# Six marks in a table of twenty for a half-array score product, with new planner numbers and reordered first and last transfers, in a fused attention and gated feed-forward kernel

## The chip, the cores and the metric

The kernel runs on one core of one Trainium2 chip. The metric is the device time of one execution in microseconds; for the kernel before it is the median of three timed runs. One further execution was recorded by the hardware profiler, and all rows below are from that one.

The engines: TensorE (PE; its weight loads are shown apart as PEld), VectorE (DVE), ScalarE (ACT), GpSimd (POOL) and SyncE (SP), which here only issues transfers. Each engine works through its own list of instructions in a fixed order.

## The reference

```python
scores = scale * np.matmul(q, k.transpose(0, 1, 3, 2))      # 8 batches, 8 heads, 576 x 64; scale = 1/8
thresh = np.max(scores, axis=-1, keepdims=True) - tau
scores = np.where(scores >= thresh, scores, -1000000000.0)
scores = scores - np.max(scores, axis=-1, keepdims=True)
attn = np.exp(scores)
attn = attn / (np.sum(attn, axis=-1, keepdims=True) + 1e-09)
attn_out = np.matmul(attn, v)
...
x = attn_out with the heads side by side                     # 8 x 576 x 512
h = np.maximum(x @ w_in, 0.0)                                # 1024 channels
conv_out = a depthwise convolution of h over 3 neighbouring tokens (conv_w)
gate = 1.0 / (1.0 + np.exp(-conv_out))
return h * gate @ w_out                                      # 8 x 576 x 512
```

All in float32.

## The kernel before, in words

**Tiling.** A batch has 576 query rows: four tiles of 128 and one of 64. They form two chunks, tiles 0 and 1, and tiles 2, 3 and 4. The eight heads are taken as four pairs. A *unit* is one tile of one pair; a batch has 20 units, 8 in its first chunk and 12 in its second, and in every odd pair the tiles of a chunk are walked backwards. `unit` makes the scores of both heads in PSUM (tiles `ps_s`, two buffers, one head each), then the largest score of a row (DVE, `top`), the exponential (ACT, `exp`), a limit (`limit`), the mask with the row's sum (DVE, `mask`), a few small steps on the sums, and the normalisation (`norm`, POOL). `transposes` turns the result on PE (tiles `ps_t`), ACT copies it out to `eT`, and `attend` multiplies by v: first a product on quarters of the array (`mixed`), then four on halves of its columns. From batch 1 on, `attend` does two pairs together.

**Precision.** Batch 0 computes its scores in plain float32, on halves of the array's rows (line 537). Later batches split q and k into upper and lower bits (`q1`, `q2`; k's upper bits of a head stand in 64 partitions of `ks` and its lower bits in the other 64) and multiply with 128 rows: `q1` and `q2` each meet the upper and the lower bits of k at once (line 544, four products of 288 columns per head). The 64-row tile stays in float32 (line 537) in every batch.

**Feed-forward.** `mm1` multiplies a chunk's 256 or 322 columns by w_in (line 713, three products per 128 rows), DVE, ACT and POOL make convolution and gate, and a lower-bit rest `gl` is written by `low`. `mm2` multiplies 128 tokens by w_out (line 786). The feed-forward of a chunk is spread over the units of the next chunk. The weights come in 16 pieces of 512 KB, and each is rounded by ACT, POOL and three DVE instructions (lines 372 to 378).

**What sets the order.** Every step is given to a planner (`Plan`) with an engine, an assumed duration, a rank less an `AHEAD` value, and a kind. The planner walks through time and writes, engine by engine, a fixed order. Some steps may go to another engine if the backlog of their own is above `BACKLOG`. For PE it prefers a step of the kind that ran last (`rows`: halves or quarters of the array's rows; `cols`: halves of its columns; `turn`: transposes; `full`), within the limits in `KEEP`. So a change of one number can move instructions everywhere.

**Start and end.** The first pair's k comes in two parts on ACT's queue, its q in two parts on SP's queue, and three weight pieces follow on ACT's queue. At the end `mm2` of the last 128 tokens is copied out by ACT in one piece, and SP stores it.

## Time and profile before

| what | value |
|---|---|
| timed runs | 1109.76, 928.27, 928.84 us; median 928.84 us |
| the profiled execution's own time | 925.54 us |
| its span | 923.8 us |
| PE, DVE, ACT, POOL busy | 97%, 80%, 76%, 63% of the span |
| instructions | 19667 |

The span is the time from the first to the last instruction in the trace; 1.7 us of the execution's own time lie outside it. Busy shares are averages over the whole span: they say which engine is worth a look, and not where it waits.

### The profile page before, as it was taken

To read this page: it belongs to the slowest core of one execution; us is meant where nothing else is said; L and a number is where in the kernel's file an instruction comes from. 1 tells how busy PE (TensorE), PEld (TensorE's weight loads), DVE (VectorE), ACT (ScalarE), POOL (GpSimd) and SP (SyncE) were. 2 spreads that over 40 slices of the span, in tenths; PEclk is the share of its full clock that TensorE was granted. 3 is DMA by queue.
4 is the path that set the end of the run, shared out by engine and by line. 5 is a ranking of instruction groups with operands and counts; after the bars stand their busy time and mean duration, and the time that the engine had idled before them with its cause. 6 is when DMAs were issued, how large, how long until landed. Compare 5 with 4: busy or idle time off the path is not lost.

```text
span 923.8 us, 19667 instructions
## 1 busy us (share of the span) xinstructions
PE 896.7 (97%) x6308; PEld 731.8 (79%) x6308; DVE 741.1 (80%) x1853; ACT 701.2 (76%) x1590; POOL 582.1 (63%) x1028
## 2 busy tenths in 40 slices
PE   5989899999999999999999999999999999999998
PEld 2446588878889788879888787887888888887897
DVE  5988999979868798878967789886977879896643
ACT  5888898878678787869768687786958788785653
POOL 3665887767747586666746677675865757664422
PEclk9999999999999999999999999999999999999999
DMA  6643363355341652345423453416523265221000
GB/s 211 200 151 128 97 166 101 111 146 167 87 122 40 176 150 83 84 115 140 122 91 81 133 148 103 120 59 166 161 85 95 55 175 140 83 79 60 13 24 34
DMA packets 77926, 104.02 MB, mean 113 GB/s; under 512 B 18560, under 2 KB 49536, under 8 KB 77824
## 3 DMA queue, kind: packets, MB, share of 16 engines
q1 hardware_dynamic: 76960, 100.86, 38.6%
q10 hardware_dynamic: 864, 1.90, 0.6%
q8 instruction: 51, 0.84, 0.4%
q14 instruction: 51, 0.42, 0.1%
HBM read 58.88 MB, written 9.44 MB: 74 GB/s over the span
## 4 chain that ended last, share of the span: by engine, by line
PE 79%; ACT 9%; DVE 6%; issue 2%; DMA 2%; POOL 1%; SPq 0%; ACTq 0%; POOLq 0%; DVEq 0%
PE po L786 21%; PE ph L713 16%; PE ps_t L626 13%; PE pa L685 12%; PE ps_s L544 11%; PE ps_s L537 4%; ACT eT L621 2%; PE pa L676 2%; DVE em L564 2%; ACT em L561 2%; DVE few L552 1%; DVE t L748 1%; PE pw_stage L394 1%; DMA q<-in_qd_dram 1%; ACT hp L728 1%
## 5 line engine op out<-in xcount | busy, mean ns | idle before, releaser
L597 POOL TENSOR_SCALAR em<-em,few 128x576 f32<-128x576 f32 x285 | 258.3, 914 | 36.9 <-DVE few L588 27.3
L564 DVE SCALAR_TENSOR_TENSOR em<-ps_s,few,em 128x576 f32<-128x576 f32 x288 | 228.1, 812 | 51.0 <-ACT em L561 44.9
L713 PE MATMUL ph<-x,w1h 128*128 128x322 f32 (+1 forms) x1024 | 243.2, 305 | 0.7 <-ACT hp L728 0.7
L552 DVE TENSOR_REDUCE few<-ps_s 128x1 f32<-128x576 f32 x288 | 210.8, 748 | 29.4 <-PE ps_s L537 15.2
L561 ACT ACTIVATE em<-ps_s,few 128x576 f32<-128x576 f32 x288 | 206.7, 743 | 30.9 <-DVE few L552 26.0
L621 ACT ACTIVATE eT<-ps_t 128x512 f32<-128x512 f32 (+2 forms) x416 | 203.3, 512 | 16.9 <-PE ps_t L626 15.2
L626 PE MATMUL ps_t<-ident,em 128*128 128x128 f32 x1312 | 187.7, 276 | 4.6 <-DVE x L695 1.7
L626 PEld LDWEIGHTS ps_t<-ident,em 128*128 128x128 f32 x1312 | 152.3, 141 | 34.2 <-POOL em L597 11.0
L713 PEld LDWEIGHTS ph<-x,w1h 128*128 128x128 f32 x1024 | 174.9, 189 | 3.7 <-issue 1.8
L748 DVE SCALAR_TENSOR_TENSOR t<-hp,cw,t 128x255 f32<-128x255 f32 (+1 forms) x256 | 151.9, 597 | 25.9 <-ACT t L732 18.8
L544 PE MATMUL ps_s<-ks,q 128*128 128x288 f32 x896 | 155.0, 304 | 2.6 <-DVE em L564 1.6
L713 PE MATMUL ph<-x,w1l 128*128 128x322 f32 (+1 forms) x512 | 151.1, 295 | 0.0
L544 PEld LDWEIGHTS ps_s<-ks,q 128*128 128x128 f32 x896 | 129.0, 188 | 13.8 <-issue 4.6
L324 POOL TENSOR_TENSOR gl<-t,gh 128x255 fp32r<-128x255 f32 (+9 forms) x192 | 121.4, 644 | 29.4 <-ACT gh L765 29.2
L685 PE MATMUL pa<-eT,v 128*64 128x320 f32 (+1 forms) x1024 | 133.3, 412 | 0.0
L685 PEld LDWEIGHTS pa<-eT,v 128*64 128x64 f32 x1024 | 70.9, 138 | 59.9 <-issue 16.7
L786 PE MATMUL po<-w2h,gh 128*128 128x512 f32 x288 | 118.1, 410 | 0.0
L786 PE MATMUL po<-w2h,gl 128*128 128x512 f32 x288 | 113.0, 392 | 0.5 <-POOL gl L324 0.5
L786 PE MATMUL po<-w2l,gh 128*128 128x512 f32 x288 | 113.1, 393 | 0.0
L713 PEld LDWEIGHTS ph<-x,w1l 128*128 128x128 f32 x512 | 96.6, 189 | 0.1
L755 DVE SCALAR_TENSOR_TENSOR t<-t,hp 128x321 f32<-128x321 f32 (+1 forms) x128 | 70.8, 554 | 14.3 <-ACT t L757 13.6
L757 ACT ACTIVATE t<-t 128x321 f32<-128x321 f32 (+1 forms) x128 | 56.9, 445 | 24.4 <-DVE t L748 24.1
(69 smaller groups left out, 1019.6 us busy)
## 6 DMA issues: line engine op xcount, KB each, us to landing
q<-q SPq DMA_DIRECT2D x336, 64.0 KB, 2.0
v<-in_vc_dram SPq DMA_DIRECT2D x64, 288.0 KB, 3.3
k<-in_kp_dram SPq DMA_DIRECT2D x35, 320.0 KB, 3.6
out_dram<-ot SPq DMA_DIRECT2D x36, 256.0 KB, 2.0
xk<-in_kt_dram SPq DMA_DIRECT2D x28, 288.0 KB, 3.3
ks<-xk SPq DMA_DIRECT2D x56, 144.0 KB, 2.4
xq<-in_qt_dram SPq DMA_DIRECT2D x56, 128.0 KB, 2.3
stage<-in_w_out_dram SPq DMA_DIRECT2D x8, 512.0 KB, 3.5
```

The costliest lines, as they stand in the source:

```text
L324: engines[e].tensor_tensor(dst, x, y, op=ALU.subtract)
L544: nc.tensor.matmul(ps[:, c, :CH], lhsT=q[:, h, o:o + n], rhs=k[:, h, c * CH:(c + 1) * CH], start=(i == 0), stop=(i == 1))
L552: nc.vector.tensor_reduce(few[:rows, nm], ps[:rows, :, :CH], op=ALU.max, axis=mybir.AxisListType.XY, negate=True)
L561: nc.scalar.activation(view(), ps[:rows, :, :CH], AF.Exp, bias=few[:rows, nm])
L564: nc.vector.scalar_tensor_tensor(view(), ps[:rows, :, :CH], few[:rows, th], view(), op0=ALU.is_ge, op1=ALU.mult, accum_out=few[:rows, total])
L597: engines[e].tensor_scalar(sl, sl, by, to, op0=ALU.mult, op1=ALU.add)
L621: "act", act(w, True), lambda dst=dst, src=src: nc.scalar.activation(dst(), src(pt), AF.Copy),
L626: nc.tensor.transpose(out=pt[:, at:at + P], in_=em[:, int(b * P):int(b * P) + P], identity=ident[:])
L685: nc.tensor.matmul(pa[j * D:(j + 1) * D, :w], lhsT=vt[:, blk, :], rhs=eT[:, blk, :w], start=False, stop=(r == 3))
L713: nc.tensor.matmul(ph[:, :an], lhsT=w1[w][:, cb, fs], rhs=xs[cb][:, h, :an], start=(cb == 0 and i == 0), stop=(cb == NCB - 1 and i == 2))
L748: nc.vector.scalar_tensor_tensor(t[:, :kn], hp[:, k:kn + k], cw[:, 3 * f + k:3 * f + k + 1], t[:, :kn], op0=ALU.mult, op1=ALU.add)
L786: nc.tensor.matmul(po[:], lhsT=x[:, f, at:at + P], rhs=w[:, f, :], start=(f == 0 and i == 0), stop=(f == NFB - 1 and i == 2))
```

## The change

It has four parts.

**The half-array product.** A table `ROWS` of 20 marks, one for each unit of a batch, has six ones. Where a mark is set and the unit has split q and k, `q1` meets k as before (`mm_high`, two products per head), and `q2` meets only the upper bits of k (`mm_low`): four products on 64 of the array's rows, the two heads on different halves. The product of the two lower parts is left out there. Both `ps_s` buffers are begun before `mm_low` closes them. The ones stand at places 1, 4, 9, 11, 15 and 16. At places 10, 11, 16 and 17 of a batch the unit is the 64-row tile, which has no split q, so the marks at 11 and 16 do nothing: the built program has 112 instructions of `mm_low` (line 553), which is 28 units, four in each of seven batches.

**First transfers.** The second part of the first pair's k goes to SP's queue, between the two parts of q; all weight pieces go to SP's queue.

**Last output.** The last 512 columns are copied out in two halves, by ACT and DVE, and stored by ACT's and SP's queues.

**Planner numbers.** `AHEAD`, `BACKLOG`, `ALT`, `KEEP`, `MOE`, `TAP` and `LOW` have new values, with separate ones (`AHEAD0`, `BACKLOG0`) for the first 24 ranks. `NORM` names DVE in its first entry, which `NEAR = 0` never reads. In the built program this moves 25 of the `gl` subtractions (`low`) and 38 of the small steps on the sums from POOL to DVE; 32 first convolution taps (`tap0`) from POOL to ACT; 18 limits from DVE, and 19 from ACT, to POOL; and 3 normalisations from ACT to POOL.

```diff
-AHEAD = {'s': 6.25, 's4': 7.75, 't': 3.5, 'a': 3.5, 'prep': 4.25, 'w': 2.5, 'load': 7.75}
+
+AHEAD = {'s': 6.25, 's4': 7.25, 't': 4.25, 'a': 4.0, 'prep': 5.0, 'w': 2.0, 'load': 8.0}
+AHEAD0 = {'s': 6.25, 's4': 7.75, 't': 3.5, 'a': 3.5, 'prep': 3.0, 'w': 2.5, 'load': 8.75}
+HEAD = 24
...
-TAP = ('act', 'pool', 'act', 'act')
-LOW = ('pool', 'pool')
+TAP = ('act', 'act', 'act', 'act')
+LOW = ('pool', 'pool', 'pool', 'dve')
...
-MOE = (2, 2)
-BACKLOG = {'pool': 6860.0, 'dve': 120.0, 'act': 9000000000.0}
+MOE = (2, 1)
+BACKLOG = {'pool': 19208.0, 'dve': 60.0, 'act': 9000000000.0}
+BACKLOG0 = {'pool': 13720.0, 'dve': 120.0, 'act': 9000000000.0}
...
-ALT = 11.76
+ALT = 5.88
...
+ROWS = (0, 1, 0, 0, 1, 0, 0, 0, 0, 1, 0, 1, 0, 0, 0, 1, 1, 0, 0, 0)
...
-KEEP = {'rows': 2.304, 'cols': 1.613, 'turn': 3.226, 'full': 2.304}
+KEEP = {'rows': 2.304, 'cols': 1.613, 'turn': 4.516, 'full': 2.304}
...
-            for j, on in enumerate((slice(0, CH), slice(CH, S + D))):
-                op(
-                    "act", 450, lambda on=on: nc.scalar.dma_start(k[:, on], kp[b, p, :, on]), w=[(k, j)], ahead=210 - 10 * j,
...
+            op("act", 450, lambda: load_k(nc.scalar, first), w=[(k, 0)], ahead=210, late=LATENCY["sp"] + 700)
+            op("sp", 700, lambda: load_q(0), w=[(q, 0)], ahead=210, late=700)
+            op("sp", 800, lambda: load_k(nc.sync, second), w=[(k, 1)], ahead=209, late=500)
+            op("sp", 600, lambda: load_q(1), w=[(q, 1)], ahead=208, late=500)
...
+        pss = [plan.buf(ps_s, "ps_s", 2, [P, 2, 512], F32, f"ps_s_{u}_{h}") for h in range(m)]
+
+        side = q2 is not None and ROWS[u % len(ROWS)]
+        if side:
+
+            def mm_high(h):
+                for c in range(2):
+                    nc.tensor.matmul(
+                        pss[h][:, c, :CH], lhsT=q1[:, h, o:o + n], rhs=k[:, h, c * CH:(c + 1) * CH], start=True, stop=False
+                    )
+
+            def mm_low():
+                for c in range(2):
+                    for h in range(2):
+                        on = slice(h * D, (h + 1) * D)
+                        nc.tensor.matmul(
+                            pss[h][:, c, :CH], lhsT=q2[on, h, o:o + n], rhs=k[on, h, c * CH:(c + 1) * CH], start=False, stop=True
+                        )
+
+            for h in range(2):
+                op(
+                    "pe", 267, lambda h=h: mm_high(h), w=[(pss[h], 0)], r=[(x, (h, i)) for x in (k, q1) for i in range(2)], ahead=a,
+                    kind="full"
+                )
+            op("pe", 267, mm_low, w=[(ps, 0) for ps in pss], r=[(x, (h, h)) for x in (k, q2) for h in range(2)], ahead=a, kind="rows")
...
+        x, y = slice(0, DO // 2), slice(DO // 2, DO)
+        op("act", act(DO // 2, True), lambda: nc.scalar.activation(ot[:, x], po[:, x], AF.Copy), w=[(ot, 0)], r=[(po, 0)])
+        op("dve", dve(DO // 2), lambda: nc.vector.tensor_copy(ot[:, y], po[:, y]), w=[(ot, 1)], r=[(po, 0)])
+        op("act", 450, lambda: nc.scalar.dma_start(rows[:, x], ot[:, x]), r=[(ot, 0)], late=LATENCY["sp"])
+        op("sp", sp(DO // 2), lambda: nc.sync.dma_start(rows[:, y], ot[:, y]), r=[(ot, 1)])
```

**How the order moves, first place.** SP's queue at the very start of the program, before (`k_1`, `q1_1`, `v_1` are of the second pair; `stage` is a weight piece):

```order
L460 DMA q1_0_79<-in_qd_dram 128x256 x2
L451 DMA k_1_96<-in_kp_dram 128x640
L363 DMA stage_3_107<-in_w_in_dram 128x512
L452 DMA q1_1_124<-in_qd_dram 128x2x256
L513 DMA v_0_130<-in_vc_dram 128x576
```

and now:

```order
L466 DMA q1_0_79<-in_qd_dram 128x256
L463 DMA k_0_77<-in_kp_dram 128x352
L466 DMA q1_0_79<-in_qd_dram 128x256
L373 DMA stage_0_97<-in_w_in_dram 128x512
L373 DMA stage_1_107<-in_w_in_dram 128x512
L373 DMA stage_2_119<-in_w_in_dram 128x512
L373 DMA stage_3_131<-in_w_in_dram 128x512
L458 DMA k_1_150<-in_kp_dram 128x640
L459 DMA q1_1_160<-in_qd_dram 128x2x256
```

The first pair's second part of k stands second, and four weight pieces now stand ahead of the second pair's k.

**Second place.** PE in batch 0, where the fourth pair's product with v begins, before (`ps_t` are transposes, `pa` the product with v, `k_381` the next pair's k):

```order
L626 MATMUL ps_t_4_480<-ident,em_375 128x128 x4
L626 MATMUL ps_t_8_491<-ident,em_292 128x128
L626 MATMUL ps_t_8_491<-ident,em_375 128x128
L676 MATMUL pa_510<-eT_435,v_298 64x256 x2
L537 MATMUL ps_s_0_516<-k_381,q_4_400 128x288 x2
L537 MATMUL ps_s_1_523<-k_381,q_4_400 128x288 x2
L685 MATMUL pa_510<-eT_435,v_298 64x256 x8
```

and now:

```order
L664 MATMUL ps_t_4_479<-ident,em_384 128x128 x4
L573 MATMUL ps_s_1_486<-k_268,q_3_283 128x288 x2
L664 MATMUL ps_t_8_495<-ident,em_334 128x128
L664 MATMUL ps_t_8_495<-ident,em_384 128x128
L573 MATMUL ps_s_0_505<-k_413,q_4_460 128x288 x2
L714 MATMUL pa_514<-eT_447,v_321 64x256 x2
L723 MATMUL pa_514<-eT_447,v_321 64x256 x8
```

One score product now stands between the last transposes and the product with v that reads them.

**Third place.** PE in batch 4, around a joint product with v of two pairs, before (line 544 is the score product, line 713 `mm1`):

```order
L544 MATMUL ps_s_1_5971<-ks_1_5650,q_33_5709 128x288
L544 MATMUL ps_s_1_5971<-ks_1_5650,q_33_5729 128x288
L676 MATMUL pa_5976<-eT_5611,v_5601 64x320 x2
L676 MATMUL pa_5979<-eT_5744,v_5627 64x320 x2
L685 MATMUL pa_5976<-eT_5611,v_5601 64x320 x8
L685 MATMUL pa_5979<-eT_5744,v_5627 64x320 x8
L626 MATMUL ps_t_0_6042<-ident,em_5770 128x128 x4
L713 MATMUL ph_5_6052<-x_4800,w1h 128x256
```

and now, at a marked unit (lines 545 and 553 are `mm_high` and `mm_low`):

```order
L545 MATMUL ps_s_1_5856<-ks_0_5679,q_32_5489 128x288 x2
L553 MATMUL ps_s_0_5845<-ks_0_5679,q_32_5514 128x288
L553 MATMUL ps_s_1_5856<-ks_0_5679,q_32_5514 128x288
L553 MATMUL ps_s_0_5845<-ks_0_5679,q_32_5514 128x288
L553 MATMUL ps_s_1_5856<-ks_0_5679,q_32_5514 128x288
L714 MATMUL pa_5870<-eT_5595,v_5562 64x320 x2
L714 MATMUL pa_5873<-eT_5687,v_5577 64x320 x2
L723 MATMUL pa_5870<-eT_5595,v_5562 64x320 x8
L723 MATMUL pa_5873<-eT_5687,v_5577 64x320 x8
L664 MATMUL ps_t_0_5931<-ident,em_5814 128x128 x4
L580 MATMUL ps_s_0_5940<-ks_1_5702,q_33_5712 128x288
```

The half-array products stand directly ahead of the product with v, and the next scores close behind it; so it is at 27 of the 28 marked units.

## Rows read from the trace of the kernel before

**Rows 1.** The page's busy times: engine, busy us, share, instructions.

```profile
PE 896.7 (97%) x6308; PEld 731.8 (79%) x6308; DVE 741.1 (80%) x1853; ACT 701.2 (76%) x1590; POOL 582.1 (63%) x1028
```

**Rows 2.** Busy time by stage, granted PE clock, DMA share and GB/s.

```profile
0.00:20.00 20.00, 10.23 (x36) 4.96 (x36) 10.11 (x26) 9.76 (x18) 6.91 (x21) 1.00 0.74 243
20.00:106.00 86.00, 76.47 (x478) 45.34 (x478) 78.22 (x187) 71.53 (x149) 54.13 (x82) 0.96 0.46 145
106.00:858.00 752.00, 747.84 (x5417) 627.73 (x5415) 624.24 (x1586) 585.89 (x1341) 499.21 (x881) 1.00 0.41 113
858.00:924.00 66.00, 62.20 (x382) 53.81 (x380) 28.53 (x59) 34.00 (x86) 21.88 (x45) 0.99 0.07 25
```

**Rows 3.** PE's timeline in batch 4: start, duration, instruction, count, [idle before <- releaser].

```profile
502.26 1.60 PE L544 MATMUL ps_s<-ks,q 128*128 128x288 f32 x8 [1.18 <-DVE em L564]
```

**Rows 4.** PE's timeline in the first microseconds.

```profile
4.56 1.33 PE L537 MATMUL ps_s<-k,q 64*128 64x288 f32 x4 [4.56 <-ACT q L466]
7.47 1.33 PE L537 MATMUL ps_s<-k,q 64*128 64x288 f32 x4 [1.58 <-ACT em L561]
10.48 2.30 PE L537 MATMUL ps_s<-k,q 64*128 64x288 f32 x8 [1.68 <-DVE em L564]
```

**Rows 5.** An issue on ACT's queue, then issues by line: count, size, us to landing.

```profile
1.70 0.39 ACTq L456 DMA_DIRECT2D k<-in_kp_dram  x1
...
stage<-in_w_in_dram ACTq DMA_DIRECT2D x3, 512.0 KB, 8.6
...
k<-in_kp_dram ACTq DMA_DIRECT2D x1, 176.0 KB, 5.6
k<-in_kp_dram ACTq DMA_DIRECT2D x1, 144.0 KB, 3.0
```

**Rows 6.** DVE's timeline at the start.

```profile
8.84 0.76 DVE L552 TENSOR_REDUCE few<-ps_s 128x1 f32<-128x576 f32 x1 [1.90 <-PE ps_s L537]
...
17.04 0.67 DVE L375 SCALAR_TENSOR_TENSOR stage_f<-stage,stage_f 128x512 uint32<-128x512 uint32 x1
```

**Rows 7.** PE's timeline in batch 0, 21 to 47 us.

```profile
21.77 0.76 PE L537 MATMUL ps_s<-k,q 64*128 64x288 f32 x4
22.45 1.13 PE L394 MATMUL pw_stage<-stage_f,ident 128*128 128x512 f32 x2
...
25.01 1.95 PE L685 MATMUL pa<-eT,v 128*64 128x256 f32 x16
...
36.11 1.24 PE L537 MATMUL ps_s<-k,q 64*128 64x288 f32 x8
37.28 1.09 PE L626 MATMUL ps_t<-ident,em 128*128 128x128 f32 x8
38.21 1.02 PE L394 MATMUL pw_stage<-stage_f,ident 128*128 128x512 f32 x2
...
44.33 0.65 PE L676 MATMUL pa<-eT,v 64*64 64x256 f32 x4 [1.85 <-ACT eT L621]
...
46.61 3.11 PE L685 MATMUL pa<-eT,v 128*64 128x256 f32 x16
```

**Rows 8.** PE's timeline in batch 4, around two heads' scores.

```profile
464.33 1.21 PE L544 MATMUL ps_s<-ks,q 128*128 128x288 f32 x8
465.38 0.39 PE L786 MATMUL po<-w2h,gh 128*128 128x512 f32 x1
```

**Rows 9.** Groups by line and shape: busy us, mean ns of one, idle before.

```profile
L732 ACT ACTIVATE t<-hp,cw 128x321 f32<-128x321 f32 x48 | 27.2, 567 | 2.6 <-POOL gl L324 0.7
...
L695 DVE TENSOR_TENSOR x<-pa,x 128x256 fp32r<-128x256 f32 x32 | 13.4, 418 | 18.1 <-ACT x L692 18.1
...
L581 DVE TENSOR_SCALAR few<-few 128x2 f32<-128x2 f32 x50 | 12.3, 245 | 1.4
```

**Rows 10.** The last output copy; a copy of half its width; store sizes and landing.

```profile
920.29 0.60 ACT L793 ACTIVATE ot<-po 128x512 f32<-128x512 f32 x1 [4.89 <-PE po L786]
...
L692 ACT ACTIVATE x<-pa 128x256 fp32r<-128x256 f32 x32 | 12.1, 379 | 21.4 <-PE pa L685 21.4
...
out_dram<-ot SPq DMA_DIRECT2D x36, 256.0 KB, 2.0
```

More of the change, by code (lines that the diff above doesn't have):

```diff
@@ L567, in mask @@
                 )
-            op(
-                "pe", 490 if q2 is None else 534, mm, w=[(ps, 0)],
-                r=[(x, j) for x in (k, q1) for j in js] if q2 is None else [(x, (h, i)) for x in (k, q1, q2) for i in range(2)], ahead=a, kind="rows" if q2 is None else "full"
-            )
+            if not side:
+                op(
+                    "pe", 490 if q2 is None else 534, mm, w=[(ps, 0)],
+                    r=[(x, j) for x in (k, q1) for j in js] if q2 is None else [(x, (h, i)) for x in (k, q1, q2) for i in range(2)],
+                    ahead=a, kind="rows" if q2 is None else "full"
+                )
             op("dve", 668, top, w=[(few, ("nm", h))], r=[(ps, 0)], ahead=a)
@@ L616, in group @@
             op(
[L617 removed]
+                "pe", width * 0.852, lambda: parts(pt), w=[(pt, 0)], r=reads + [(ident, 0)], ahead=lead("t"), kind="turn"
             )
```

65 lines of the change are left out of this document (34 added, 31 removed).

## The prediction

> **What bounds the kernel now.** The first view is the page's table of busy times [rows 1]: PE is busy for 896.7 of 923.8 us, so the reader should ask where the other 27 us lie, and not which other engine could be faster. The second view, the stages [rows 2], answers that. From 106 to 858 us PE is idle for 752.00 - 747.84 = 4.2 us in all, at a granted clock of 1.00. From 0 to 20 us it is idle for 9.8, from 20 to 106 us for 9.5, and there the clock is 0.96. After 858 us about 3.6 us are left, nearly all of it behind PE's last instruction. So three things can move the time: PE's own work in the main stage, the 19 us of idleness before 106 us, and the tail. The third view is PE's own waits in the main stage; the longest is 1.18 us, for a mask on DVE [rows 3]. The fourth view, the timeline of the first microseconds, shows what the early idleness is made of [rows 4 to 6]. PE makes the first head's scores at 4.56 us and the second's at 7.47 us. The row blames an exponential, but the second part of k was issued at 1.70 us on ACT's queue and took 5.6 us to land, which gives 7.3 us: PE waits for that transfer. DVE then idles 1.90 us before its second maximum, and all that follows is late by as much.
>
> **The change, part by part.** The sum is made against the profiled execution's own 925.54 us; the median of the three timed runs, 928.84, is 3.3 us above it, and I add that at the end.
>
> *The half-array product.* A unit's scores take eight products: 465.38 - 464.33 = 1.05 us [rows 8], 0.131 us each. In a marked unit four remain (0.52 us). The four half-array products take 2 x 0.131 = 0.26 us if two run side by side, and 4 x 0.131 = 0.52 us, as much as before, if each runs alone. The trace has no split product on half the array; the nearest rows are float32 ones on 64 rows. Eight of them take 37.28 - 36.11 = 1.17 us, and a single group of four 22.45 - 21.77 = 0.68 us, so a group costs 0.49 us and a stay in that kind 0.19 to 0.21 us on top [rows 7]. That is 0.12 us for 288 columns, while eight full float32 products of 128 columns take 38.21 - 37.28 = 0.93 us, or 0.116 us for 128 columns. Per column the half ones cost less than half: they run in pairs. I take 0.26. The order has 28 such units, not the 42 that six marks in twenty would give, since two marks fall on 64-row tiles. 28 x (1.05 - 0.52 - 0.26) = 7.5 us less on PE.
>
> *What they cost in changes of kind.* By the count of the order PE enters the kind "rows" 53 times before and 68 times now. The half-array products don't add an entry by themselves, because 27 of 28 stand directly ahead of the product with v, which is of that kind; but the 64-row tiles' scores, which stood there, now often stand alone. 15 x 0.21 = 3.2 us more. Between `mm_low` (64 rows, 128 columns) and the product with v (64 by 64) the array is divided anew. No row shows that step; it costs between nothing and a whole stay of 0.21 us, I take 0.1, and 27 of them are 2.7 us. PE's work is then 7.5 - 3.2 - 2.7 = 1.6 us less; between 7.5 less (no change of kind costs anything) and 8.9 more (products one by one, 3.2 and 5.7 for the changes). The Trainium skill, "TensorEngine Tiling", section Key Properties, says that changing the tiling mode, and not merely the tile, drains the engine. The 0.2 us of a stay agree with it; by it each of the 27 steps would cost the full 0.21 us, 5.7 us in all, PE would do 1.4 us more work in place of 1.6 less, and the forecast would be 924.4 us.
>
> *First transfers.* The second part of k now stands second on SP's queue, ahead of all weights. The part of 144 KB that went out first landed in 3.0 us [rows 5]; with an issue at about 1.1 us this one lands between 4.1 and 5 us, before PE is done with the first head at 4.56 + 1.33 = 5.9 us. The second head then starts 7.47 - 5.9 = 1.6 us earlier, and DVE's 1.90 us go with it. What is late next is DVE. Its order shows that the rounding of two weight pieces (six instructions, some 0.6 us each by the row at 17.04 us [rows 6]) now stands ahead of the second pair's first maximum, where one instruction stood: about 3 us of work done earlier, in time that was idle. From 20 to 106 us DVE is busy for 78.22 of 86 us [rows 2], so what it has done by 20 us counts at the end of that stage. I take 3.5 us. Against it: 2 MB of weights now stand ahead of the second pair's k on SP's queue. At 243 GB/s with 0.74 of the queues' time in use, full use is some 330 GB/s; the 3.2 MB up to and with the second pair's q need 10 us and land at 11 to 12 us. Before, PE reached that pair at 15 us, and now it has eight transposes and a weight product ahead of it. That covers the landing; without cover PE would wait 2 us. Weights landing late would also hold ACT, which has a weight step between the first two exponentials, by up to 2 us. Ends: 6 less, 2 more.
>
> *The rest of batch 0.* At 44.33 us PE waits 1.85 us for a copy of transposes, and after it the clock falls: the same 16 products take 3.11 us at 46.61 us and 1.95 us at 25.01 us [rows 7], which is 1.2 GHz in place of 2.4 for a while. The new order puts a score product of 0.5 to 0.7 us between the transposes and their reader, so a wait of some 1.2 us is left, and similar waits make up the 9.5 us. The new numbers for the first 24 ranks could as well open others. I take 2 us less; ends 6 less (two thirds of the stage's idleness), 4 more.
>
> *Work between engines.* DVE gets 25 subtractions and 38 small steps and loses 18 limits: 25 x 0.418 + 20 x 0.245 = 15 us [rows 9]. ACT gets 32 taps of up to 0.567 us, 18 us, less some 8 us for 19 limits and 3 normalisations. POOL loses some 30 us. In the main stage DVE is busy for 624 of 752 us and ACT for 586 [rows 2]: both stay under PE, which covers this work. What it costs if that cover is thin is more waits such as that of 1.18 us. I take nothing; ends 3 less (of the 4.2 us of waits), 8 more.
>
> *Last output.* A copy of half the width takes 0.379 us, where the whole takes 0.60; the store of 256 KB lands in 2.0 us [rows 10], and half of it will not take longer, but a second issue on ACT's queue can add 0.3. I take 0.3 us less; ends 0.6 less, 0.3 more.
>
> The sum: 1.6 + 3.5 + 2 + 0.3 = 7.4 us less, 918.1 us for the profiled execution and 921.4 us for the median.
>
> **The rivals.** *The half-array products don't pair up.* Then they save nothing, and the changes of kind remain: PE's work grows by up to 8.9 us, and 921.4 + 1.6 + 8.9 = 931.9 us, slower than before but within 2%. For it: a pair of split products writes two PSUM buffers in turn and each needs a weight load of its own. Against it: the float32 pairs [rows 7]. It decides from 7.4 us, that is 0.26 us per unit. The Trainium skill, "TensorE: Matmul & The Clock Gate", section LDWEIGHTS, gives a load as columns over 1.2 GHz, whatever the rows, 107 ns here; as an estimate by it four loads one after another make the half-array part 0.43 us long, and the time 926 us. The same page lets loads to different rows of the array overlap, and no run here shows which.
>
> *The score buffers are held too long.* A marked unit begins both `ps_s` buffers and closes them only with `mm_low`, which often waits for the product with v: in the order products of the feed-forward lie between, on average some 4 us of PE's work, up to 9. In that time DVE and ACT get no scores. Behind the product with v the next scores ask for the same buffers at once. If the mask isn't ready, PE waits as it did at 502.26 us, 1.18 us [rows 3]. 28 x 1.18 = 33 us gives 954 us, the slow side. It makes the kernel slower than before from 0.26 us per unit, and by 2% from 0.93 us. Against it: the product with v covers about 4 us, and the next two masks need some 3 to 3.5 us from the last product; PE waited for masks in the main stage a few times only.
>
> *The start heals altogether.* If most of the 19 us of idleness before 106 us goes, all but the first 4.56 us and some 4 us of the first softmax, 11 us are won, with 3 us from the clock that stays up: 925.5 - 14 - 1.6 - 0.3, and 3.3 for the median, is 913 us. With changes of kind that cost nothing it is 907.
>
> **How the numbers follow.** The forecast has a chance of 0.55, products that don't pair 0.17, held buffers 0.08, a healed start 0.20. The forecast's own range, with the ends of its terms half used, is 914 to 930. The whole range takes in a part of the healed start and the unpaired products: 911 to 933 us. Two per cent, which is about what a measurement of this kernel can tell from no change, are 18.6 us: faster means under 910.3, slower over 947.4. A third of the healed start and a sliver of the forecast lie under 910.3: 0.09. About half of the held buffers' cases lie over 947.4: 0.04. The rest, 0.87, is the same.
>
> **What would show it.** In the profile after: line 553 with 112 products and pairs that start within some ns of each other, and a marked unit of 0.8 us; PE's second head before 6.2 us and the second pair's scores not waiting for k; PE idle under 7 us from 0 to 20 us; the main stage still with under 6 us of idle time; the last copy at 0.4 us. The forecast is wrong if PE waits for masks behind line 723, if line 553 takes 0.5 us per unit, or if batch 0 keeps its idle time.

## The result

The changed kernel takes 930.88 us (median of 18 runs, 929.06 to 932.08) and the kernel before, run in turn with it, 926.85 us: a ratio of 1.0045 (95% interval 1.0035 to 1.0055), 4 us slower. The prediction said 921.4 us and a gain of 7.4, on a median of 928.84 us that the longer series puts at 926.85. The time lies inside the range of 911 to 933 us and inside 2% of the kernel before, but on the other side of it. The profiled execution took 931.15 us, with a span of 929.3 us.

The busy times of the changed kernel, which answer to [rows 1]:

```profile
PE 902.9 (97%) x6308; PEld 723.6 (78%) x6308; DVE 771.8 (83%) x1899; ACT 714.3 (77%) x1600; POOL 557.0 (60%) x973
```

PE is busy for 6.2 us more, and the span is 5.5 us longer: the loss lies in PE's busy time and not in its waiting. The same stages as in [rows 2]; columns: length of the stage, busy us of PE, PEld, DVE, ACT and POOL, granted PE clock, DMA share, GB/s:

```profile
0.00:20.00 20.00, 11.48 (x36) 5.56 (x37) 11.31 (x25) 10.80 (x19) 8.68 (x22) 1.00 0.72 230
20.00:106.00 86.00, 75.95 (x477) 45.29 (x477) 80.11 (x180) 70.10 (x148) 58.24 (x90) 0.97 0.48 150
106.00:858.00 752.00, 747.77 (x5388) 614.50 (x5388) 644.53 (x1620) 594.68 (x1339) 471.18 (x824) 1.00 0.40 113
858.00:930.00 72.00, 67.74 (x412) 58.29 (x411) 35.89 (x78) 38.68 (x97) 18.89 (x40) 1.00 0.06 23
```

In the main stage PE idles for 752.00 - 747.77 = 4.2 us, as before. The two stages ahead of it keep their idle time: 8.5 and 10.1 us, where 9.8 and 9.5 stood. PE's work behind 858 us is 67.74 instead of 62.20 us: the last stage shows what had not been done by then.

Another cut is the first split score product, where the scores of batch 1 begin. It starts at 116.75 us before and at 119.36 us now. From there to the end of the span it is 807.0 us before and 809.9 now. So the start is 2.6 us longer (the forecast had 5.5 less) and the rest 2.9 us (the forecast had 1.9 less). The 2.6 us are less sure than they look. Four of the kernels below have the order of the changed kernel up to this point, engine by engine, or that of the kernel before: the changed order starts its split scores at 119.4, 118.9, 117.7 and 117.8 us, the old one at 116.8 and 118.2, so the means lie 1 us apart. And six products of `mm2`, the output of the feed-forward, stand ahead of the cut that stood behind it before; they are 1.4 us of work. What is sure is that the gain of 5.5 us isn't there. PE's timeline of the start, beside [rows 4]:

```profile
3.86 1.33 PE L573 MATMUL ps_s<-k,q 64*128 64x288 f32 x4 [3.86 <-ACT q L477]
5.97 1.33 PE L573 MATMUL ps_s<-k,q 64*128 64x288 f32 x4 [0.78 <-ACT q L477]
...
12.74 1.97 PE L664 MATMUL ps_t<-ident,em 128*128 128x128 f32 x8 [0.71 <-POOL em L635]
15.81 2.08 PE L401 MATMUL pw_stage<-stage_f,ident 128*128 128x512 f32 x2 [1.10 <-DVE stage_f L388]
16.90 1.42 PE L402 MATMUL pw_stage<-w1h,minus 128*128 128x512 f32 x1
18.24 1.70 PE L573 MATMUL ps_s<-k,q 64*128 64x288 f32 x8
```

The second head does come 1.5 us earlier, as forecast. But the second pair's scores begin at 18.24 us, behind eight transposes and a weight product that itself waits 1.10 us for DVE. In the kernel before they began at 14.91 us:

```profile
14.91 1.33 PE L537 MATMUL ps_s<-k,q 64*128 64x288 f32 x4
```

The transfers behind the second head, beside [rows 5]:

```profile
stage<-in_w_in_dram SPq DMA_DIRECT2D x8, 512.0 KB, 5.7
...
k<-in_kp_dram SPq DMA_DIRECT2D x1, 176.0 KB, 3.5
k<-in_kp_dram ACTq DMA_DIRECT2D x1, 144.0 KB, 2.8
```

PE's timeline at two places ahead of the first split score and at a marked unit of batch 4, beside [rows 7] and [rows 8]:

```profile
43.53 0.76 PE L573 MATMUL ps_s<-k,q 64*128 64x288 f32 x4 [0.92 <-ACT q L477]
44.21 0.65 PE L714 MATMUL pa<-eT,v 64*64 64x256 f32 x4
44.79 1.95 PE L723 MATMUL pa<-eT,v 128*64 128x256 f32 x16
...
104.25 0.88 PE L664 MATMUL ps_t<-ident,em 128*128 128x128 f32 x4 [2.81 <-POOL em L635]
...
459.66 0.39 PE L824 MATMUL po<-w2l,gh 128*128 128x512 f32 x1
459.98 0.53 PE L553 MATMUL ps_s<-ks,q 64*128 64x288 f32 x4
460.44 0.66 PE L714 MATMUL pa<-eT,v 64*64 64x256 f32 x8
461.03 3.67 PE L723 MATMUL pa<-eT,v 128*64 128x256 f32 x32
```

The wait of 1.85 us at 44 us and the half clock behind it are gone: the 16 products take 1.95 us, at the higher of the two levels. But another has come: the transposes at 104.25 us have waited 2.81 us for a normalisation on POOL, and the granted clock is 0.5 for the next 3.4 us. The kernel before has two such stretches of 3.4 us ahead of its first split score, at 45.6 and 72.9 us, and the changed kernel two, at 70.4 and 104.5 us.

A half-array part takes 0.46 us from its start to the next instruction's (0.460 to 0.464 at all 28 units), where 0.26 was forecast, and the product in front of it gives way after 0.32 us, where such products do after 0.23. The end of the program, beside [rows 10]:

```profile
925.35 0.39 PE L824 MATMUL po<-w2l,gh 128*128 128x512 f32 x1
925.83 0.38 ACT L838 ACTIVATE ot<-po 128x256 f32<-128x256 f32 x1 [4.89 <-PE po L824]
926.24 0.35 ACTq L840 DMA_DIRECT2D out_dram<-ot  x1
926.24 0.42 DVE L839 COPY ot<-po 128x256 f32<-128x256 f32 x1 [11.02 <-ACT ot L838]
926.69 0.33 SPq L841 DMA_DIRECT2D out_dram<-ot  x1
```

DVE's copy begins when ACT's ends: the program makes it wait for the semaphore of ACT's copy. Each half's store lands in 1.7 us, and the end of the span stands 3.56 us behind PE's last instruction, where it stood 3.55 before.

### The profile page after: what moved, and what is told of

Same layout as the page of the kernel before. It is cut to its first block, busy times and chain, and to the rows that moved or that the text cites. A ratio compares the mean times of both kernels' runs of the same rounds, so it can differ in the third digit from the quotient of the medians.

```text
span 929.3 us, 19789 instructions
## 1 busy us (share of the span) xinstructions
PE 902.9 (97%) x6308; PEld 723.6 (78%) x6308; DVE 771.8 (83%) x1899; ACT 714.3 (77%) x1600; POOL 557.0 (60%) x973
## 4 chain that ended last, share of the span: by engine, by line
PE 80%; DVE 7%; ACT 5%; DMA 3%; issue 2%; POOL 2%; SPq 0%; ACTq 0%; DVEq 0%; POOLq 0%
PE po L824 20%; PE ph L751 17%; PE ps_t L664 13%; PE pa L723 12%; PE ps_s L580 9%; DVE em L600 3%; PE ps_s L573 3%; PE pa L714 2%; DMA q<-in_qd_dram 2%; DVE few L588 2%; ACT em L597 1%; ACT eT L659 1%; PE ps_s L545 1%; PE ps_s L553 1%; POOL em L635 1%
## 5 line engine op out<-in xcount | busy, mean ns | idle before, releaser
L635 POOL TENSOR_SCALAR em<-em,few 128x576 f32<-128x576 f32 x288 | 262.6, 920 | 51.0 <-DVE few L626 34.2
L600 DVE SCALAR_TENSOR_TENSOR em<-ps_s,few,em 128x576 f32<-128x576 f32 x288 | 228.3, 812 | 22.8 <-ACT em L597 16.7
L659 ACT ACTIVATE eT<-ps_t 128x512 f32<-128x512 f32 (+2 forms) x416 | 200.9, 510 | 33.7 <-PE ps_t L664 31.7
L664 PE MATMUL ps_t<-ident,em 128*128 128x128 f32 x1312 | 194.4, 277 | 5.8 <-POOL em L635 4.6
L786 DVE SCALAR_TENSOR_TENSOR t<-hp,cw,t 128x255 f32<-128x255 f32 (+1 forms) x256 | 160.9, 632 | 34.3 <-ACT t L770 32.2
L334 POOL TENSOR_TENSOR gl<-t,gh 128x255 fp32r<-128x255 f32 (+14 forms) x167 | 107.3, 654 | 29.3 <-ACT gh L803 28.9
L580 PE MATMUL ps_s<-ks,q 128*128 128x288 f32 x672 | 120.1, 307 | 3.8 <-DVE em L600 2.2
L580 PEld LDWEIGHTS ps_s<-ks,q 128*128 128x128 f32 x672 | 97.1, 189 | 17.1 <-issue 8.6
L793 DVE SCALAR_TENSOR_TENSOR t<-t,hp 128x321 f32<-128x321 f32 (+1 forms) x128 | 66.2, 518 | 12.5 <-ACT t L795 11.9
L770 ACT ACTIVATE t<-hp,cw 128x321 f32<-128x321 f32 (+1 forms) x128 | 69.1, 540 | 4.0 <-POOL gl L334 1.5
```

The costliest lines, as they stand in the source:

```text
L334: engines[e].tensor_tensor(dst, x, y, op=ALU.subtract)
L580: nc.tensor.matmul(ps[:, c, :CH], lhsT=q[:, h, o:o + n], rhs=k[:, h, c * CH:(c + 1) * CH], start=(i == 0), stop=(i == 1))
L600: nc.vector.scalar_tensor_tensor(view(), ps[:rows, :, :CH], few[:rows, th], view(), op0=ALU.is_ge, op1=ALU.mult, accum_out=few[:rows, total])
L635: engines[e].tensor_scalar(sl, sl, by, to, op0=ALU.mult, op1=ALU.add)
L659: "act", act(w, True), lambda dst=dst, src=src: nc.scalar.activation(dst(), src(pt), AF.Copy),
L664: nc.tensor.transpose(out=pt[:, at:at + P], in_=em[:, int(b * P):int(b * P) + P], identity=ident[:])
```

## The experiments

"Over before" is the median less that of the kernel before in the same series; the changed kernel has 4.0. The start is the time of the first split score product, the rest the span from there to the end (116.75 and 807.0 us before, 119.36 and 809.9 in the changed kernel). Both come from one profiled execution each; single executions of one kernel lie up to 7 us apart, and starts under one order up to 1.7 us. PE's idle time is given without the end behind its last instruction.

### The half-array products

**The changed kernel without marks** (no split score product uses half the array):

```
-ROWS = (0, 1, 0, 0, 1, 0, 0, 0, 0, 1, 0, 1, 0, 0, 0, 1, 1, 0, 0, 0)
+ROWS = (0,) * 20
```

> The changed kernel with ROWS all zero: every split score product is back to four full ones per head; planner numbers, first transfers and last output as changed. PE enters the kind rows 54 times by the order, as before the change (53). Theory A, the marks are what costs (their own division of the array and 15 more stays, some 0.2 us each, and the waits that come with both score buffers held): 4 to 5 us less than the changed kernel, 926 us or a little under the kernel before. Theory C, the planner's numbers open waits (transposes waiting for normalisations): it stays at 929 to 931 us, and PE's idle time and the waits of line 664 stay as they are in the changed kernel.

Measured 936.69 us, a ratio to the kernel before of 1.0112 (1.0094 to 1.0131): 10.9 us over before, and the change is *better* with its marks than without, which neither theory had. Start 118.88, rest 816.4 us.

**The kernel before with the half-array products alone** (old numbers, transfers and output):

```
+ROWS = (0, 1, 0, 0, 1, 0, 0, 0, 0, 1, 0, 1, 0, 0, 0, 1, 1, 0, 0, 0)
...
+        side = q2 is not None and ROWS[u % len(ROWS)]
```

> The kernel before with the marks alone (same six ones, 28 units in effect); planner numbers and transfers as before. PE enters the kind rows 75 times by the order. Theory A: 22 more stays and 28 half-array parts of 0.46 us; slower than the kernel before by 3 to 6 us, and DVE's maxima wait for the half-array products. Theory C: within 1 us of the kernel before. If half-array products saved what they should, 5 us faster.

Measured 932.05 us, 1.0064 (1.0045 to 1.0083): 6.3 us over before. Start 118.18, rest 813.2 us. That is theory A's side, a little beyond its 3 to 6 us. The same products cost 6 us under the old numbers and give 7 back under the new ones.

**The changed kernel with every half-array product done twice** (the output is another):

```
+                for r in range(2):
                     for c in range(2):
                         for h in range(2):
```

> The changed kernel with each half-array product issued twice, so that the rest of q counts twice in the marked units; the order is otherwise the same. The part of four takes 0.46 us in the profile of the changed kernel. Theory A (two heads run side by side at 0.13 us a round, and some 0.2 us are a fixed price for dividing the array anew and loading weights into it): the part of eight takes 0.46 + 0.26 = 0.72 us, 7 us more in all. Theory B (a round takes 0.23 us on half the array, because of its columns or of its weight loads): 0.92 us, 13 us more in all.

PE's timeline at the same unit; the part is line 554 here:

```profile
458.05 0.39 PE L825 MATMUL po<-w2l,gh 128*128 128x512 f32 x1
458.37 0.79 PE L554 MATMUL ps_s<-ks,q 64*128 64x288 f32 x8
459.10 0.66 PE L715 MATMUL pa<-eT,v 64*64 64x256 f32 x8
```

Eight products take 0.72 us (0.720 to 0.730) where four take 0.46: two more rounds cost 0.26 us, 0.13 a round, so the heads do run side by side, and 0.20 us are a fixed price of the stay. This is theory A. The whole takes 932.72 us, 1.0074 (1.0053 to 1.0095), 7.0 over before: of 28 x 0.26 = 7.3 us of added work on PE only 3 show in the medians. In the profiled execution PE's idle time is 19.0 us in place of 22.8, so part of the work fills waits; where the rest went isn't shown.

**The changed kernel with full-array products in the same places.** Each engine's order stays row for row:

```
-                        on = slice(h * D, (h + 1) * D)
+                        on = slice(0, P)
```

> The changed kernel with one alteration: the four products of line 553 take all 128 rows (q2 meets upper and lower bits of k), nothing else; every engine's order stays row for row that of the changed kernel. So this prices the half-array form at a fixed order. In the changed kernel the four half-array products take 0.463 us, and the score products ahead of them end 0.09 to 0.17 us later than such products do elsewhere; the product with v behind them takes 0.592 us, as it does behind full-array products in the kernel before (0.593). Theory A, a stay on half the array costs what it saves: the four full products take 0.52 to 0.53 us, the step ahead of them loses its 0.09 to 0.17, so PE does 28 x 0.03 to 0.10 = 0.8 to 2.8 us less, and the time is 928 to 931 us beside 930.9. Theory B, the half-array form is worth what was forecast, and the order around it spoils it: 28 x 0.17 to 0.27 us more, 935 us and over.

```profile
459.24 0.39 PE L824 MATMUL po<-w2l,gh 128*128 128x512 f32 x1
459.47 0.69 PE L553 MATMUL ps_s<-ks,q 128*128 128x288 f32 x4
460.09 0.66 PE L714 MATMUL pa<-eT,v 64*64 64x256 f32 x8
```

The step in front now takes 0.23 us and the part 0.62, together 0.85, where the half-array form takes 0.32 + 0.46 = 0.78: it saves 0.07 us a unit (0.06 to 0.08 at 27 units), some 2 us in all. Measured 933.1 us, 1.0083 (1.0063 to 1.0103), 8.5 over before. So the half-array form is a gain at a fixed order, between both theories: neither its whole saving is eaten, nor is it worth the 0.17 us a unit that the forecast left it. The full products need 0.09 us before the array is divided for the product with v; the half-array ones have paid that, and 0.20 more, already.

### The first transfers

**The kernel before with the new first transfers and the last output by halves, alone**, as in the change's diff:

```
+            op("sp", 800, lambda: load_k(nc.sync, second), w=[(k, 1)], ahead=209, late=500)
...
+        op("dve", dve(DO // 2), lambda: nc.vector.tensor_copy(ot[:, y], po[:, y]), w=[(ot, 1)], r=[(po, 0)])
```

> The kernel before with the new first transfers and the last output by halves alone; marks and planner numbers as before. If the second head's earlier start is worth what the prediction said, 3 to 4 us faster, PE idle under 7 us from 0 to 20 us. If later waits in batch 0 take it back, as they seem to in the changed kernel (PE idle 8.5 us to 20 us and 10.0 us to 106 us, together 0.7 us less than before), within 1 us of the kernel before.

Measured 929.22 us, 1.0045 (1.0029 to 1.0062): 3.5 over before, where neither theory has it. Start 124.08, rest 806.3 us: all of it, and more, is the start, though some 2 us of the start are nine products of `mm2` more that stand ahead of the cut. PE's timeline there:

```profile
6.01 1.33 PE L541 MATMUL ps_s<-k,q 64*128 64x288 f32 x4 [0.51 <-ACT q L470]
...
12.63 1.97 PE L630 MATMUL ps_t<-ident,em 128*128 128x128 f32 x8 [1.30 <-POOL em L601]
...
16.40 1.42 PE L395 MATMUL pw_stage<-w1h,minus 128*128 128x512 f32 x1
17.62 2.62 PE L630 MATMUL ps_t<-ident,em 128*128 128x128 f32 x10
...
20.94 0.79 PE L395 MATMUL pw_stage<-w1h,minus 128*128 128x512 f32 x1
21.66 1.24 PE L541 MATMUL ps_s<-k,q 64*128 64x288 f32 x8
```

The second head is early here too, and the second pair's scores start 6.7 us later than before: in the order that the planner wrote with the weights first on SP's queue, two weight products and 18 transposes stand between.

**The kernel before with the second part of k alone moved**, from second on ACT's queue to SP's, behind the first part of q; every other instruction keeps its place:

```
-... lambda on=on: nc.scalar.dma_start(k[:, on], kp[b, p, :, on]), ...
+... lambda on=on, j=j: None if j else nc.scalar.dma_start(k[:, on], kp[b, p, :, on]), ...
...
+... None if j else nc.sync.dma_start(k[:, CH:], kp[b, p, :, CH:])), ...
```

> The kernel before with one transfer moved: the second part of the first pair's k is issued on SP's queue behind the first part of q, in place of second on ACT's; every other instruction keeps its place on its engine. Theory A, the early transfer is worth what was forecast and was lost only because the planner wrote another order from it: PE's second head starts at 6.0 us in place of 7.47, DVE's wait of 1.90 us goes, the first split scores start at 113 to 115 us in place of 116.75, and the time is 922 to 925 us where the kernel before has 926. Theory B, the start gives nothing that lasts, since DVE and POOL are the limit until 106 us and take up any head start in their own work: the second head is early, but the first split scores still start at 116 to 117 us and the time is that of the kernel before within 1 us.

```profile
4.58 1.33 PE L537 MATMUL ps_s<-k,q 64*128 64x288 f32 x4 [4.58 <-ACT q L466]
7.95 1.33 PE L537 MATMUL ps_s<-k,q 64*128 64x288 f32 x4 [2.04 <-ACT q L466]
```

Neither theory had this: the second head is later, not earlier. The moved part of k lands at 5.2 us, two earlier than before. But the second head's q now comes third on SP's queue, and ACT scales it at 7.48 us, when it has landed; two weight pieces, issued from 1.71 us on ACT's queue, move at the same time. In the changed kernel the weights are issued from 2.12 us, behind that q, and it is scaled at 5.51 us. Measured 926.63 us, 1.0017 (1.0000 to 1.0033), 2.0 over before.

### The planner numbers

**The kernel before with the new numbers alone**, all those of the change, with the planner's assumed time of a transfer (`SPW`):

```
+AHEAD = {'s': 6.25, 's4': 7.25, 't': 4.25, 'a': 4.0, 'prep': 5.0, 'w': 2.0, 'load': 8.0}
...
+KEEP = {'rows': 2.304, 'cols': 1.613, 'turn': 4.516, 'full': 2.304}
```

> The kernel before with the new planner numbers alone: no half-array products, the old first transfers, the old last output. Theory A, the parts add, and the numbers are the dear one: the kernel without marks took 936.7 us and the first transfers alone 3.5 us, so 933 us here, with the waits of transposes for the exponential's copies and the normalisation (after 110 us) near 10 us in place of 2.5. Theory B, the numbers are harmless by themselves and suffer only under the new first transfers: 926 to 928 us, with those waits under 5 us.

```profile
0.00:20.00 20.00, 10.08 (x33) 4.62 (x34) 8.73 (x22) 9.39 (x20) 6.21 (x21) 1.00 0.72 243
20.00:106.00 86.00, 76.35 (x464) 44.21 (x466) 76.77 (x179) 69.19 (x143) 55.22 (x84) 1.00 0.45 139
106.00:858.00 752.00, 740.94 (x5306) 617.88 (x5306) 626.80 (x1579) 593.22 (x1338) 479.94 (x842) 0.99 0.41 113
858.00:945.00 87.00, 81.07 (x510) 67.27 (x508) 42.33 (x94) 46.21 (x110) 23.11 (x49) 0.98 0.09 29
```

Measured 944.35 us, 1.0206 (1.0184 to 1.0228): 19.7 over before, the largest price of all. Neither theory had so much. The start is 122.82, the rest 819.8 us. Columns as above: in the main stage PE idles for 11.1 us instead of 4.2, and in all it is busy for 11.7 us more.

**The changed kernel with the old BACKLOG.**

```
-BACKLOG = {'pool': 19208.0, 'dve': 60.0, 'act': 9000000000.0}
-BACKLOG0 = {'pool': 13720.0, 'dve': 120.0, 'act': 9000000000.0}
+BACKLOG = {'pool': 6860.0, 'dve': 120.0, 'act': 9000000000.0}
+BACKLOG0 = {'pool': 6860.0, 'dve': 120.0, 'act': 9000000000.0}
```

> The changed kernel with BACKLOG and BACKLOG0 set to the old values (POOL 6860, DVE 120), all else as changed. In the built program POOL hands more of its steps to ACT and DVE again. Theory A, POOL's longer backlog is what makes transposes wait for normalised masks: their waits after 110 us fall from 6.1 us to about 3, and the time to 927 or 928 us. Theory B, the loss comes from the whole set of numbers and from no single one: the waits stay within 2 us of what they were in sum (16.7 us), and the time within 1.5 us of 930.9.

Measured 930.85 us, 1.0057 (1.0040 to 1.0075): no better, as theory B has it. Start 113.32, 6 us earlier than in the changed kernel and 3.4 earlier than before, and rest 813.0 us. About 3 of the 6 us only move the cut: nine products of `mm2` and eight transposes that stand ahead of it in the changed kernel stand behind it here. So a somewhat earlier start is to be had, and the time is no shorter for it.

**The kernel before with two groups of the new numbers**: `AHEAD`, `AHEAD0` and `HEAD`, then `TAP`, `LOW`, `MOE`, `ALT`, `NORM`, `NEAR`, `BACKLOG` and `BACKLOG0`.

> The kernel before with AHEAD, AHEAD0 and HEAD alone new (all other numbers, the transfers and the products as before). In its order 103 groups of split score products stand directly behind transposes, where the kernel before has 51 and the kernel with all new numbers 98; four such products take 0.61 us there and 0.53 us behind feed-forward products. Theory A, the leads are what makes the numbers dear: 52 x 0.08 = 4.3 us more on PE and as much again in waits, 934 to 942 us, most of the 18 us that all numbers cost. Theory B, the leads are harmless and the steps' places among the engines (TAP, LOW, MOE, BACKLOG) are dear: 926 to 930 us.

> The kernel before with TAP, LOW, MOE, ALT, NORM, NEAR, BACKLOG and BACKLOG0 alone new. 70 groups of split score products stand behind transposes. Theory A (the leads are the dear part): 19 x 0.08 = 1.5 us more on PE, 927 to 931 us. Theory B (the places are the dear part, since DVE and ACT take over some 30 us from POOL): waits for masks on DVE and for ACT's copies, 935 to 944 us.

The leads: 929.67 us, 1.0041 (1.0026 to 1.0056), 3.8 over before. The places: 932.27 us, 1.0070 (1.0049 to 1.0091), 6.4 over. The first is where theory B has it, the second a little beyond theory A's range and well below theory B's, so neither group is the dear one: 3.8 and 6.4 don't make 19.7. `KEEP` and the assumed time of a transfer, the rest of the numbers, were not run alone.

### What any new order costs

**Nudges**: one number of the planner is moved a little, the work is the same. In the kernel before, PE's assumed latency to 220 and to 200 ns, and the lead of the weights to 2.6:

```
-LATENCY = {"pe": 210.0, ...}
+LATENCY = {"pe": 220.0, ...}
...
-AHEAD = {..., 'w': 2.5, ...}
+AHEAD = {..., 'w': 2.6, ...}
```

> The kernel before with one assumed latency of the planner changed from 210 to 220 ns (PE's), nothing else: the same work, the same engines but for a few small steps, in another order (in most of the list PE's rows stand in other places). Theory A, any new order of this kernel costs some us, since the order before was chosen among many: 928 to 934 us where the kernel before has 925 to 926, with PE's waits and changes of kind a little up. Theory B, an order is as good as the numbers behind it, and 10 ns change nothing: 925 to 926.5 us.

> The kernel before with the planner's lead of the weights changed from 2.5 to 2.6, nothing else: a nudge of another place, which moves instructions in the first fifth of the program alone. Theory A, any new order costs: 927 to 932 us. Theory B, such a nudge changes nothing: within 1 us of the kernel before.

> The kernel before with PE's assumed latency 200 ns in place of 210: the third nudge. Theory A, the order before is the best of many, and any other costs: 928 to 933 us, like the nudges to 220 (930.4) and of the weights' lead (931.0). Theory B, those two were unlucky: 924 to 927 us.

Measured 930.39 us, 1.0049 (1.0031 to 1.0068), for 220 ns; 930.97 us, 1.0056 (1.0036 to 1.0077), for the lead; 926.87 us, 1.0017 (1.0007 to 1.0028), for 200 ns. Ten nanoseconds in an assumption cost 4.5 us; two of the three are theory A's (any new order costs), the third is theory B's.

The same three nudges of the changed kernel (its early lead `AHEAD0` for the weights):

> The changed kernel with PE's assumed latency 220 ns in place of 210, nothing else. Theory A, the change itself is worth about nothing, its order is one among many: the time lies anywhere between 927 and 935 us, and the mean of the three nudged changed kernels is within 2 us of the mean of the three nudged kernels before (some 931). Theory B, its parts cost by themselves: 3 to 6 us more than the nudged kernels before, 934 to 937 us.

> The changed kernel with PE's assumed latency 200 ns, nothing else. Theory A (the order alone): 927 to 935 us. Theory B (the parts cost by themselves): 934 to 937 us.

> The changed kernel with the early lead of the weights 2.6 in place of 2.5, nothing else, the counterpart of the nudge of the kernel before that cost 5.1 us. Theory A (the order alone): 927 to 935 us. Theory B (the parts cost by themselves): 934 to 937 us.

Measured 936.2 us, 1.0115 (1.0098 to 1.0131); 934.8 us, 1.0100 (1.0082 to 1.0118); 931.35 us, 1.0062 (1.0046 to 1.0078). The first is theory B's (the parts cost by themselves), the second lies in both ranges, the third in theory A's (the order alone). The nudged changed kernels lie 11.1, 9.7 and 6.3 us over before, the nudged kernels before 4.5, 5.1 and 1.8. On the mean of three orders the change costs 5.2 us, more than the 2 us that theory A allowed, though three orders that differ by up to 5 us among themselves fix such a mean only roughly. Each kernel's own order has the lowest time of its four; for the changed kernel the third nudge is within the noise of it.

### The two missing combinations

**The marks and the numbers, without the transfers and the output; the marks with the transfers and the output, under the old numbers.**

> The changed kernel with the old first transfers and the old last output: half-array products and planner numbers alone. Theory A, prices of the parts add up: 18.4 + 6.3 = 24.7 us over the kernel before, 950 us. Theory B, the numbers suit marks (they took 5.8 us off with the new transfers): 18.4 - 5.8 = 12.6, 938 us. Theory C, each combination is one order among many, and the 18.4 us of the numbers alone were a bad one: 4 to 9 us over, 929 to 935 us.

> The kernel before with the half-array products, the new first transfers and the last output by halves, under the old planner numbers. Theory A, prices add up: 6.3 + 3.5 = 9.8 us over, 935 us. Theory B, marks are worth something beside the new transfers only: 3.5 - 5.8, 923 us, faster than the kernel before. Theory C, one order among many: 2 to 9 us over, 927 to 934 us.

Measured 937.25 us, 1.0137 (1.0116 to 1.0158), and 934.34 us, 1.0097 (1.0081 to 1.0114). With these all eight combinations are known, in per cent over the kernel before:

| | neither | marks | transfers | both |
|---|---|---|---|---|
| old numbers | 0 | 0.64 | 0.45 | 0.97 |
| new numbers | 2.06 | 1.37 | 1.12 | 0.45 |

Under the old numbers marks cost 0.64 and 0.52, transfers 0.45 and 0.33. Under the new ones marks gain 0.69 and 0.67, transfers 0.94 and 0.92. Within a row the prices add up; between the rows they change sign. The first run is theory B's (938 expected), the second theory A's (935). Each cell is a single order, and nudges alone move a kernel by 0.2 to 0.7%, so the single steps, and the neatness with which they add up, may be chance; the 2.06 and the way back to 0.45 are larger than any nudge.

## Why the prediction was wrong

**The failed steps, in short.** The 5.5 us that the forecast took off for the first transfers and the rest of batch 0 did not come. A half-array product saves 0.07 us, where 0.17 was counted. And the count of changes of kind took in only PE's entries into the kind "rows"; 32 more steps from transposes to full products, 0.08 us each, stand in no term. That the time lies inside 911 to 933 us owes to the width of that range and not to the mechanism, and that it lies 1 us from the unpaired products' 931.9 us is luck: the products do pair.

**What held.** PE bounds the kernel. The heads' half-array products run side by side; 27 of 28 parts stand ahead of the product with v; the entries into "rows" grew by 15; the second head is early; the wait at 44 us and the half clock behind it went. The weight loads of a pair start 3 to 4 ns apart and those of the second pair 108 ns later: the prediction's estimate with four loads one after another, 0.43 us, comes near the 0.46 measured, but it isn't what happens. The held score buffers cost PE next to nothing: DVE waits for them, and PE does not:

```profile
L588 DVE TENSOR_REDUCE few<-ps_s 128x1 f32<-128x576 f32 x288 | 208.9, 748 | 44.2 <-PE ps_s L553 31.9
```

**The half-array product, mis-sized.** The forecast gave a marked unit a saving of 0.27 us and took 0.1 us back for dividing the array anew, from ends of 0 and 0.21. The rows give a saving of 0.07 us in place of 0.17: the stay costs its whole fixed price of 0.20 us, and the first part of the product with v behind it (256 columns) takes 0.592 us, as behind full-array products (0.593), not 0.542 as behind the float32 scores on half the array. The upper end was the right one. The Trainium skill, "TensorEngine Tiling", section Key Properties, says that a change of the tiling mode drains the engine; the 0.20 us, with no discount behind the split products, are in line with it. The difference is 28 x 0.10 = 2.8 us.

**Changes of kind, counted on one side only.** The forecast priced 15 more entries into "rows" at 0.21 us each. They are cheaper: where the 64-row tile's scores now stand alone, between a product with v and transposes, they hold PE for 1.13 us, where they held it for 1.02 directly ahead of a product with v. That is 0.11 us more at 13 places. But it left out the steps from transposes to full products. PE's timeline in batch 4:

```profile
471.28 1.03 PE L664 MATMUL ps_t<-ident,em 128*128 128x128 f32 x8
472.07 0.77 PE L580 MATMUL ps_s<-ks,q 128*128 128x288 f32 x4
472.69 0.38 PE L664 MATMUL ps_t<-ident,em 128*128 128x128 f32 x2
...
474.63 0.48 PE L824 MATMUL po<-w2h,gh 128*128 128x512 f32 x1
474.94 0.40 PE L824 MATMUL po<-w2h,gl 128*128 128x512 f32 x1
...
476.84 0.40 PE L824 MATMUL po<-w2l,gh 128*128 128x512 f32 x1
477.07 0.70 PE L580 MATMUL ps_s<-ks,q 128*128 128x288 f32 x4
477.61 0.39 PE L824 MATMUL po<-w2h,gh 128*128 128x512 f32 x1
```

Behind transposes four score products hold PE for 472.69 - 472.07 = 0.62 us, behind a feed-forward product for 0.54. A feed-forward product pays the same: 0.31 us behind transposes (474.63), 0.23 elsewhere (476.84). The planner's table prices the step from transposes to full products at 5 ns. From the first split score on PE takes this step 212 times before and 244 times now; 32 times 0.08 are 2.6 us. The marks bring most of it: it is 239 times in the kernel before with the marks alone, 226 with the numbers alone, 227 in the changed kernel without marks. (Split scores alone mislead here: 51 groups of them stand behind transposes before, 84 now and 98 with the numbers alone, where fewer feed-forward products do.)

**The sum again.** PE's busy time misses its forecast by 7.8 us (1.6 less, 6.2 more). Of the 6.2 us, 3.4 lie ahead of the first split score, 1.4 of them the six products of `mm2`. Behind it, PE is busy for 2.8 us more, and for the same work, without those six, for 4.2 us more. The rows explain 28 x 0.07 = 1.9 less, 13 x 0.11 = 1.4 more and 2.6 more, together 2.1 more; the other 2 us there, and the 2 us ahead, were not traced to one cause.

**Work between engines, taken at nothing.** The forecast asked only whether DVE and ACT stay under PE. They do, though DVE's busy time grew by 30.7 us, where 15 were forecast, and PE's waits in the main stage are as before. But alone the same numbers cost 19.7 us, far outside the ends of 3 less and 8 more: 11.7 us more busy time of PE, and 7.2 us more waits. So the term came out near nothing in the changed kernel beside the other parts only, for which the forecast had no reason.

**First transfers and batch 0: right in place, wrong in effect.** The second head came early. The forecast named the eight transposes and the weight product that now stand ahead of the second pair, and took them for the cover under which its k lands. They are that (its k landed at 13.3 us and its q at 13.9, where 11 to 12 was reckoned), but they also delay its scores by 3.3 us. The wait at 44 us was won as forecast and lost again at 104 us, with the half clock behind it; the prediction's own sign of being wrong, that batch 0 keeps its idle time, came. With the old `BACKLOG` the split scores start at 113.3 us, about half of which is a shift of the cut, so at most a part of the forecast's gain is shown to be possible. For the last output the forecast took 0.3 us less: it overlooked that the two copies of one PSUM tile stand one behind the other.

**What was shown, and what not.** Shown is that the new numbers cost about 19 us alone and that with both other parts beside them about 15 us of it go, where these two parts lose 9 under the old numbers: a price read for one part alone does not carry over. That the three were fitted to each other is the likely reason, and not shown. Shown is too that each of three nudges of the order before loses (1.8 to 5.1 us), so that a change has to win that first. Not settled is which numbers make the 19 us, and why marks change sign with them; PE's idle time falls from 28.5 to 22.8 us by the marks under the new numbers and transfers and stays (23.5 and 23.9) under the old ones. No kernel tried beats the kernel before.

## What to carry to other kernels

Where a planner writes the order, find out first what a nudge costs: move one assumption by a few per cent, and take the spread (here 2 to 7 us, all on the slow side) as a term of every forecast, with a mean that is not zero if the order before was picked among many. Read a stage's length from several executions with one order before giving a difference of 1 or 2 us a cause. Price an edit at a fixed order (replace instructions in their places), and test parts of a change in all combinations before speaking of the worth of one. In a kernel that one engine bounds, moved work on that engine has a price of its own, by its neighbours, even where every other engine stays under it: count every kind of step that the new order adds, and not only the one that the edit names.

## What the runs showed of the hardware

- Half-array products of two heads start 1 to 4 ns apart and take 0.13 us a pair for 288 columns, so the array does run both halves at once; 0.20 us of each stay are fixed.
- A full product behind transposes takes 0.08 us longer than behind another full product, scores (0.62 and 0.54 us for four) and feed-forward products (0.31 and 0.23 us) alike.
- The part of the product with v on quarters of the array (256 columns, two pairs) takes 0.59 us behind half-array split products and 0.54 behind half-array float32 ones: both are products on 64 rows, and only the second saves its entry.
- The second part of q, 128 KB issued at 1.64 or 1.65 us, was scaled at 7.48 us where two weight pieces were issued on the other queue from 1.71 us, and at 5.51 us where the weights were issued behind it on its own queue from 2.12 us: its place on its own queue did not protect it from the other one. How much of the 2 us the 0.4 us later issue makes isn't shown.
- At the start PE's products take nearly twice as long as later, and the order alone doesn't set the moment of the change: four transposes take 1.11 us at 16.17 us and 0.66 us at 18.70 us in the kernel before, and still 1.11 us at 18.84 us in the kernel before with the marks alone, which has the same order there. The first product with v then starts at 23.74 us in the one and at 25.37 us in the other. The granted clock reads 1.00 up to there in both.
